# Row sums in the place of unread matmuls, and a second output piece that begins in another PSUM bank

## The chip, the cores and the metric

The kernel runs on one core of a Trainium2 chip. The core has four compute engines that this text names: TensorE (PE; its weight loads are PEld), VectorE (DVE), ScalarE (ACT) and GpSimd (POOL). SyncE (SP) issues most of the DMAs. The metric is the time of one execution in microseconds (us) on the device.

## The reference

Two computations follow one another. The first is a gated recurrence over 5056 tokens, for 4 sequences and 256 channels. The second is a soft mixture of experts on all 4 x 5056 = 20224 resulting tokens, with 8 experts of 4 slots, so 32 slots.

```
f = lower_bound + (1 - lower_bound) * sigmoid(f_logit)
h[t] = f[t] * h[t-1] + (1 - f[t]) * x[t]          # per sequence and channel
logits = h @ phi                                  # 20224 x 32
slot_input = softmax(logits over tokens).T @ h    # 32 x 256
slot_out[e] = relu(slot_input[e] @ w1[e]) @ w2[e] # 256 -> 1024 -> 256
out = softmax(logits over slots) @ slot_out       # 20224 x 256
```

The inputs x and f_logit have 20.7 MB each, the weights of the experts 16.8 MB in all, and the output has 20.7 MB. All of them are float32.

## The kernel before

The tokens of each sequence are cut into 10 groups (`n_grp`) of up to 512, so that 40 units (`n_unit`) of one group of one sequence arise. The order of all instructions is written out by hand (`tc.manual_schedule()`): each engine works through its own instructions in that order, and waits only for the data that it needs.

The loop over the units (from line 471) is a software pipeline. It loads six units ahead on SyncE's queue (L202 to L216). ScalarE takes the sigmoid (L226), GpSimd multiplies it with x (L237), TensorE transposes both to channels (L246 to L258), ScalarE makes the decay (L286, L293), and VectorE runs the recurrence as a scan (L304). TensorE transposes the result back to tokens (L317), VectorE or ScalarE copies it (L334), and TensorE forms the logits (L348). ScalarE takes their exponential into `etall` (L357), which stays in SBUF for the whole kernel, with a row for each sequence and slot and a column for each token. After a transpose of these weights (L369, copied in L372) TensorE sums the weighted tokens into `slot_ps` (L398). GpSimd's queue issues the 16 loads of the experts' weights along the way, at units that `W_AT` lists (L130, L140). These loads convert to bfloat16. The last two experts' `w2` go into a buffer of `f_t` (the tile `w_t`), and the very last comes in three parts: a half and two quarters.

In several places the loop calls `idle(k)` (L171): k matmuls of the 128 x 128 identity with 256 columns, which write into the second half of the bank of `slot_ps`. Nobody reads what they write. `spin(dst, k, w)` (L143) does the like with k matmuls of w columns of the first expert's weights. It is called after the loop, and writes into `tail[:, 1]`.

`tail` (L528) is a PSUM tile of 2 x 512 float32, so of two banks of 2 KB each. Its first bank holds `rs_ps`, the sums over the 32 slots for each token, and in the kernel before also `sin_ps`. Its second bank holds two transposes that are done by then, and the unread results of `spin`.

`row_sums(i)` (L377) is a matmul per 128 tokens, of the weights with four columns of ones (`ones`), and gives the denominators of the second softmax. The tokens of a sequence lie in blocks for it: two blocks of 2048 tokens (16 matmuls each) and one of 896 (7 matmuls), and 64 tokens are left over, for which L384 has a matmul of its own.

After the loop come the experts. `slot_sb` is a copy of `slot_ps` (L583). L587 brings it to channels in `sin_ps`. VectorE and ScalarE scale it into `sin` (L598, L599), TensorE multiplies with `w1` (L615), and ScalarE and VectorE apply the relu (L620, L622). TensorE transposes (L630); the first four experts go through `hid` (L651), the last four through `wide` (L664, a loop over j). Within this last loop the row sums are formed, and VectorE inverts them into `rrow` (L674, L680, L681). The scaled slots are `slot_out` (L683, L684) and `slot_bd` (L686).

The output stage multiplies `etall` with the slots. `pieces` (L714) treats the first 2048 tokens of sequence 0 in small pieces, so that the first store can start early: in each pair of pieces VectorE divides one (`by_vector`, L694) and ScalarE the other (`by_scalar`, L698), and each is then stored (L730). The sizes are (1, 2), (3), (2), counted in rows of 256 floats. For each entry of the list there is a new pair of PSUM tiles `op` of two banks each, and the pieces of one entry follow one another in the same tile, at the place `at`. `couple` (L744), `rest` (L770) and `whole` (L733) treat the remaining output in larger parts.

Of the kernel before, what the change touches and what calls it, by code (L numbers as in the profile page):

```python
# [18 lines left out]
def kernel(  # L19
# [11 lines left out]
    B, S, D = x.shape  # L31
    E = moe_w1.shape[0]
    F = moe_w1.shape[2]
    NS = moe_phi.shape[1]
    SPE = NS // E
    P = 128
    DC = D // P
    FC = F // P
    R = 4
    G = P * R  # L40
# [19 lines left out]
    wide_r = 4 * R  # L60
# [84 lines left out]
            nc.tensor.matmul(dst[:, ds(0, w)], w1_sb[0][:, 0, :P], w1_sb[0][:, 0, :w],  # L145
                             start=True, stop=True, skip_group_check=True)

    SPINS = 7
    W_AT = {9: 1, 17: 1, 25: 1, 31: 1, 32: 1, 33: 2, 34: 3, 36: 6}
    w_next = [0]  # L150
    ctx.enter_context(tc.manual_schedule())
# [4 lines left out]
    with tc.tile_pool(name="sp2", bufs=3) as sp2, \  # L156
# [217 lines left out]
            for i, k in enumerate(gs):  # L374
                ets[k] = et[:, i]

        def row_sums(i):  # L377
            t0, n_r = blocks[i]
            ew = etall[:, ds(t0, P * n_r)].rearrange("s (p r) -> s p r", r=n_r)
            for r in range(n_r):  # L380
                nc.tensor.matmul(rs_ps[:, t0 // P + r], ew[:, :, r], ones,
                                 start=True, stop=True, skip_group_check=True)
            if i == len(blocks) - 1:
                nc.tensor.matmul(rs_ps[:, n_grp * R - 1, ds(0, B // 2)],  # L384
                                 left.rearrange("s t u -> s (t u)"), pair_ones,
                                 start=True, stop=True, skip_group_check=True)
# [84 lines left out]
        for n in range(n_unit):  # L471
            if n < SINGLE - 2:
                if n:
                    unit(to_tokens, n - 1)
                    unit(u_to_channels, n + 1)
                s_to_channels(n + 2)
                if n + 3 < SINGLE:
                    gate(n + 3, 1)
                decay(n + 2, 1)
                if n + 3 == SINGLE:  # L480
                    gate(n + 3)
                if n % 2 == 0:
                    unit(load, n + AHEAD)
                unit(enter, n + 3)
                rep_constants(n)
            else:
                end = n >= n_unit - 6
                if n % 2 == 0:
                    unit(load, n + AHEAD)
                    if n == SINGLE - 2:  # L490
                        to_tokens(n - 1)
                        keep_tokens(n - 1)
                    if not end and n >= SETTLED:
                        unit(gate, n + 4)
                else:
                    unit(decay, n + 1)
                    if n < SETTLED:
                        gate(n + 3)
                    if n == n_unit - 5:
                        gate(n + 3)  # L500
                        exps(odd - 1)
                if not end and n != n_unit - 7:
                    group(exps, n - 2)

                unit(enter, n + 3)
                for _ in range(W_AT.get(n, 0)):
                    load_w(w_next[0])
                    w_next[0] += 1

                if n == n_unit - 2:  # L510
                    unit(u_to_channels, n + 1)
                if n != SINGLE - 2:
                    unit(to_tokens, n - 1)
                if n == n_unit - 2:
                    keep_tokens(n - 1)
                if n % 2 == 0:
                    unit(s_to_channels, n + 2)
                    unit(s_to_channels, n + 3)
                if n != n_unit - 2:
                    unit(u_to_channels, n + 1)  # L520
                if n in (n_unit - 5, n_unit - 4):
                    idle(8)
                elif n == SINGLE - 2:
                    idle(4, True)
                elif n < n_unit - 4 and n % (2 * B) in (1, 5, 6, 7):
                    idle({6: 8, 7: 9}.get(n, 5 if n % 2 else 4))
                if n == n_unit - 2:
                    tail = psp.tile([P, 2, G], F32, name="tail", tag="sp")  # L528
                    rs_ps = tail[:, 0, ds(0, n_grp * R * B)].rearrange(
                        "p (q b) -> p q b", b=B)  # L530
                    late_ps, odd_ps = (
                        tail[:, 1].bitcast(BF16)[:, ds(i * R * P, R * P)].rearrange(
                            "p (r s) -> p r s", r=R) for i in range(2))
                    logits(odd)
                    exps(odd)
                    slots(odd - 1)
                    spin(tail[:, 1], 1, G)
                    odd_weights()
                elif not end and long(n - 1):
                    if n % B == 0:  # L540
                        g = (n - 1) // (2 * B) * 2
                        for i in range(2):
                            logits(g + i, [2, 3] if n % (2 * B) == 0 else [0, 1])
                elif not end:
                    group(logits, n - 1)
            if n == n_unit - 1:
                logits(last, [0, 1, 2])
                late_exps([0, 1, 2])
                idle(4)
                late_weights([0, 1, 2], nc.scalar.copy)  # L550

            unit(scan, n)
            if n not in (SINGLE - 2, n_unit - 2):
                unit(keep_tokens, n - 1)
            if n == n_unit - 3:
                weights_to_tokens(odd - 1)
                slots(odd - 2)
            elif not n >= n_unit - 6:
                group(weights_to_tokens, n - 3)
                batch(slots, n - 4, 0)  # L560
                batch(slots, n - 4, 1)
                if n > 2 * B and n % (2 * B) == 3:
                    idle(6)
        hid, wide = (ld.tile([P, 2, R, D], F32, name=i, tag="x_t") for i in ("hid", "wide"))
        hid = hid.rearrange("p u r d -> p (u r d)").bitcast(BF16)[:, ds(0, FC * E // 2 * NS)]
        wide = wide.rearrange("p u r d -> p (u r d)").bitcast(BF16)[:, ds(0, FC * E // 2 * P)]
# [10 lines left out]
        slots(odd)  # L577
        late_slots([0, 1, 2])
        late_slots([3])
        spin(tail[:, 1], 21, P // 2)  # L580
        slot_sb = hpool.tile([P, G, DC], BF16, name="slot_sb", tag="h")
        slot_sb = slot_sb.rearrange("p t o -> p (t o)").bitcast(F32)[:, ds(0, D)]
        nc.vector.tensor_copy(slot_sb, slot_ps)  # L583
        sin_ps = tail[:, 0, ds(G // 2, DC * NS)].rearrange("p (o s) -> p o s", o=DC)
        slot_v = slot_sb.rearrange("p (c o) -> p o c", o=DC)
        for o in range(DC):
            nc.tensor.matmul(sin_ps[:, o], slot_v[:, o], rep[:, 0],  # L587
# [2 lines left out]
    with tc.tile_pool(name="ew", bufs=1) as ew, \  # L590
# [2 lines left out]

        rep2 = rep.rearrange("p b s -> p (b s)")

        spin(tail[:, 1], 21, P // 2)
        sin = ew.tile([P, DC, NS], BF16, name="sin")
        nc.vector.tensor_scalar_mul(sin[:, 0], sin_ps[:, 0], omlb[:, ds(0, 1)])  # L598
        nc.scalar.activation(sin[:, 1], sin_ps[:, 1], ACT.Copy, scale=omlb[:, ds(1, 1)])  # L599
# [61 lines left out]
        for j in range(Q):  # L661
            for fc in range(FC):
                for c in range(2):
                    nc.tensor.matmul(so_ps[c], wide[:, fc, j].rearrange("p b s -> p (b s)"),  # L664
                                     w2_sb[Q + j][:, fc, ds(c * C, C)],
                                     start=j == 0 and fc == 0,
                                     stop=j == Q - 1 and fc == FC - 1,
                                     skip_group_check=True)
            if j == 0:
                for c in range(2):  # L670
                    nc.tensor.matmul(so_ps[c], rep2, so4[:, ds(c * C, C)], start=False,
                                     stop=False, skip_group_check=True)
                row_sums(0)
                nc.vector.reciprocal(rrow[:, :wide_r], rs_ps[:, :wide_r])  # L674
            if j == 1:
                for i in range(1, len(blocks)):
                    row_sums(i)
                q = n_grp * R - 1
                spin(tail[:, 1], SPINS, D)
                nc.vector.reciprocal(rrow[:, wide_r:q], rs_ps[:, wide_r:q])  # L680
                nc.vector.reciprocal(rrow[:, q, ds(0, B // 2)], rs_ps[:, q, ds(0, B // 2)])  # L681
        spin(tail[:, 1], 4, D)
        nc.vector.tensor_scalar_mul(slot_out[:, ds(0, C)], so_ps[0], rcs)  # L683
        nc.scalar.activation(slot_out[:, ds(C, C)], so_ps[1], ACT.Copy, scale=rcs)  # L684
        for u in range(2):
# [4 lines left out]
    with tc.tile_pool(name="pout", bufs=4, space=PSUM) as pout, \  # L690
# [23 lines left out]
        def pieces(i, b, sizes):  # L714
            dst = rows_of(i, b)
            obs = [osb.tile([P, blocks[i][1], D], F32, name="ob", tag="ob") for _ in range(2)]
            r = 0
            for pair in sizes:
                ops = [pout.tile([P, R, D], F32, name="op", tag="op") for _ in range(2)]
                at = [0, 0]  # L720
                for k in pair:
                    todo = []
                    for j in range(2):
                        share(ops[j][:, ds(at[j], k)], i, b, r, k)
                        todo.append((r, at[j]))
                        r, at[j] = r + k, at[j] + k
                    for j, by in enumerate((by_vector, by_scalar)):
                        q, o = todo[j]
                        by(obs[j][:, ds(q, k)], ops[j][:, ds(o, k)], scale_of(i, b, q, k))
                        (nc.scalar if q == 1 else nc.sync).dma_start(  # L730
                            out=dst[:, ds(q, k)], in_=obs[j][:, ds(q, k)])
# [95 lines left out]
```

## Time and profile before

| | |
|---|---|
| runs | 200.14, 200.83 and 200.80 us; median 200.8 us |
| span of the profiled execution, first to last instruction | 198.1 us |
| its whole time | not given by the page; the runs lie 2.0 to 2.7 us above the span |
| busy: PE, DVE, ACT, POOL | 77%, 72%, 70%, 52% of the span |
| mean granted TensorE clock | 0.850 |
| DMA | 70.77 MB, mean 357 GB/s |
| chain that ended last, by engine | PE 32%, DMA 30%, DVE 18%, POOL 6% |
| `idle`, the 122 of 256 columns | 17.7 us of PE time (L174) |

The page divides the span into 40 slices, and gives the busy share of each engine and of the DMA engines in tenths, and the clock that TensorE was granted. The chain is followed back from the last instruction, at each step to what released it. A line of the timeline has the start, the length, the engine, the line of the kernel, the operation, the tiles, the number of instructions, and in brackets how long the engine had been idle and what ended that. In a line of waits stand the waiting engine and line, the one waited for, and then the total, the count and the longest in us.

### The profile page before, as it was taken

The numbers are of one execution on the slowest core, as the hardware profiler recorded it, in microseconds if no ns is written. First come the engines' busy times: TensorE is split into PE (matmuls) and PEld (weight loads), VectorE is DVE, ScalarE is ACT, GpSimd is POOL, SyncE is SP. The second block draws the span as 40 slices with busy tenths as digits, with TensorE's granted clock in tenths as the row PEclk, the third lists the DMA queues.
The fourth block names the chain that finished last, engine by engine and source line by source line (L and its number), as shares of the span: only waits on it lengthen the run. The fifth ranks groups of instructions, "written<-read, shape, count | busy, mean of one in ns | idle before, by whom it ended". The sixth has DMA issues, their size and how long they took to land.

```text
span 198.1 us, 3497 instructions
## 1 busy us (share of the span) xinstructions
PE 153.3 (77%) x1330; PEld 110.4 (56%) x1330; DVE 143.3 (72%) x164; ACT 138.7 (70%) x195; POOL 103.0 (52%) x78
## 2 busy tenths in 40 slices
PE   0587599987999989898997978999989999950000
PEld 0366478776776768676695856568953543310000
DVE  1669869999699999999989999523268878840000
ACT  2688677899889999999897595622069889980000
POOL 2489578774998688884969969290030000000000
PEclk9999759997999999999999999999995555555555
DMA  5999999999999999999999999999639999999995
GB/s 177 418 420 419 427 429 429 427 427 357 378 424 424 408 337 420 432 411 307 407 420 392 241 215 214 213 212 211 110 110 419 430 421 427 450 443 424 424 424 218
DMA packets 14448, 70.77 MB, mean 357 GB/s; under 512 B 1744, under 2 KB 3024, under 8 KB 10464
## 3 DMA queue, kind: packets, MB, share of 16 engines
q1 hardware_dynamic: 11520, 62.00, 75.5%
q0 software_dynamic: 2624, 8.42, 21.3%
q8 instruction: 10, 0.16, 0.3%
q10 hardware_dynamic: 288, 0.13, 0.2%
q14 instruction: 6, 0.05, 0.1%
HBM read 58.23 MB, written 20.71 MB: 399 GB/s over the span
## 4 chain that ended last, share of the span: by engine, by line
PE 32%; DMA 30%; DVE 18%; POOL 6%; issue 3%; ACT 1%; ACTq 0%; SPq 0%; POOLq 0%
DMA x_t<-in_x_dram 15%; DVE h L304 13%; PE op L754 12%; DMA w_t<-in_moe_w_dram 8%; DMA w_sb<-in_moe_w_dram 7%; POOL u_t L237 5%; PE hp L317 4%; PE up L258 4%; PE sp L252 3%; DVE ht L334 3%; PE op L704 2%; PE slot_ps L174 2%; PE lg L348 1%; PE slot_ps L398 1%; DVE ob L694 1%
## 5 line engine op out<-in xcount | busy, mean ns | idle before, releaser
L237 POOL TENSOR_TENSOR u_t<-s_t,x_t 128x1024 bf16<-128x1024 bf16 (+1 forms) x39 | 82.5, 2128 | 23.3 <-ACT s_t L226 13.9
L304 DVE TENSOR_TENSOR_SCAN h<-a,h,up 128x512 bf16<-128x512 f32 (+1 forms) x72 | 86.9, 1252 | 4.7 <-PE up L258 2.5
L226 ACT ACTIVATE s_t<-f_t 128x2048 bf16<-128x2048 f32 (+2 forms) x23 | 38.3, 1668 | 5.8 <-DMA f_t<-in_f_logit_dram 4.5
L317 PE MATMUL hp<-ident_f,h 128*128 128x128 f32 (+1 forms) x160 | 29.5, 309 | 7.3 <-DVE ht L334 6.0
L317 PEld LDWEIGHTS hp<-ident_f,h 128*128 128x128 f32 (+1 forms) x160 | 23.1, 208 | 15.3 <-DVE ht L334 9.6
L252 PE MATMUL sp<-ident_f,s_t 128*128 128x128 f32 x144 | 22.6, 303 | 10.1 <-ACT s_t L226 7.8
L286 ACT ACTIVATE a<-sp,nomlb 128x1024 f32<-128x1024 bf16 x24 | 25.4, 1114 | 0.8 <-PE sp L252 0.6
L252 PEld LDWEIGHTS sp<-ident_f,s_t 128*128 128x128 f32 x144 | 18.6, 158 | 11.8 <-issue 6.0
L754 PE MATMUL op<-slot_bd,etall 64*128 64x512 bf16 x62 | 24.4, 600 | 0.1
L765 ACT ACTIVATE oc<-op,rrow 128x256 f32<-128x256 f32 x60 | 22.8, 490 | 1.4 <-PE op L754 0.9
L759 DVE TENSOR_TENSOR oc<-op,rrow 128x1024 f32<-128x1024 f32 x16 | 19.3, 1223 | 4.6 <-PE op L754 4.5
L293 ACT ACTIVATE a<-sp,nomlb 128x512 f32<-128x512 bf16 (+2 forms) x22 | 17.9, 859 | 4.8 <-PE sp L252 4.4
L258 PE MATMUL up<-ident_f,u_t 64*128 64x64 f32 x192 | 17.6, 229 | 2.0 <-POOL u_t L237 1.9
L174 PE MATMUL slot_ps<-rep,ident 128*128 128x256 bf16 x122 | 17.7, 281 | 0.0
L258 PEld LDWEIGHTS up<-ident_f,u_t 64*128 64x128 f32 x192 | 13.9, 138 | 5.9 <-POOL u_t L237 2.4
L754 PEld LDWEIGHTS <-etall 64*128 64x128 bf16 x62 | 9.0, 153 | 14.2 <-issue 11.6
L334 ACT COPY ht<-hp 128x512 f32<-128x512 f32 (+1 forms) x18 | 10.4, 580 | 8.0 <-PE hp L317 7.9
L334 DVE COPY ht<-hp 128x512 f32<-128x512 f32 (+1 forms) x22 | 14.7, 668 | 0.8 <-PE hp L317 0.8
L174 PEld LDWEIGHTS <-ident 128*128 128x128 bf16 x126 | 11.4, 102 | 3.4 <-issue 1.3
L304 DVE TENSOR_TENSOR_SCAN h<-a,up 128x512 bf16<-128x512 f32 x8 | 9.3, 1209 | 2.5 <-ACT a L293 1.8
L252 PE MATMUL up<-ident_f,u_t 128*128 128x128 f32 x48 | 9.8, 337 | 0.6 <-POOL u_t L237 0.6
L348 PE MATMUL lg<-h,phi 128*32 128x512 bf16 (+1 forms) x80 | 10.0, 411 | 0.0
(105 smaller groups left out, 147.8 us busy)
## 6 DMA issues: line engine op xcount, KB each, us to landing
f_t<-in_f_logit_dram SPq DMA_DIRECT2D x12, 1024.0 KB, 12.3
x_t<-in_x_dram SPq DMA_DIRECT2D x12, 1024.0 KB, 11.4
out_dram<-oc SPq DMA_DIRECT2D x6, 2048.0 KB, 13.1
w_sb<-in_moe_w_dram POOLq DMA_DIRECT2D x14, 512.0 KB, 10.3
f_t<-in_f_logit_dram SPq DMA_DIRECT2D x12, 512.0 KB, 8.6
x_t<-in_x_dram SPq DMA_DIRECT2D x12, 512.0 KB, 9.4
out_dram<-oc SPq DMA_DIRECT2D x4, 896.0 KB, 6.1
out_dram<-ob SPq DMA_DIRECT2D x1, 2048.0 KB, 8.9
```

Of the source, the lines that this page charges most:

```text
L174: nc.tensor.matmul(slot_bank[:, 1, ds(0, rhs.shape[1])], ident, rhs, start=first and i < 2, stop=False, skip_group_check=True)
L226: nc.scalar.activation(s_t, f_t, ACT.Sigmoid, scale=-1.0)
L237: nc.gpsimd.tensor_tensor(uts[n][:, :r], s_t[:, :r], x_t[:, :r], ALU.mult)
L252: nc.tensor.transpose(ps[:, :, r], t[:, r], ident_f)
L258: nc.tensor.transpose(v[:, :, r], t(r)[k].bitcast(F32), ident_f[k, k])
L286: nc.scalar.activation(a, sp[:, :, :, :, o], ACT.Identity, scale=nomlb[:, ds(o, 1)], bias=1.0)
L304: nc.vector.tensor_tensor_scan(h[:, :T, o], decays[n // 2, o][:, n % 2, :T], up[:, :T, o], hs[number(g - 1, b)][:, ds(used(g - 1) - 1, 1), ...
L317: nc.tensor.transpose(hp[:n_p, r], hw[:, :n_p, r], ident_f)
L334: copy(hts[g][:n_p, b].rearrange("p r d -> p (r d)").bitcast(F32), hps.pop(n)[:n_p].rearrange("p r c -> p (r c)"))
L754: nc.tensor.matmul(op[:, i_r].rearrange("p u d -> p (u d)"), ew[:, :, r + i_r], slot_bd[ds(j * 2 * NS, 2 * NS)].rearrange("s u d -> s (u d)"),
L759: nc.vector.tensor_tensor(ob[:, :, ds(r, k)].rearrange("p u r d -> p r u d"), op[:, ds(0, k)], scale[:, ds(r, k)].unsqueeze(3).broadcast_t ...
L765: nc.scalar.activation(ob[:, u, r + i_r], op[:, i_r, u], ACT.Copy, scale=scale[:, r + i_r, ds(u, 1)])
```

## The change

Fewer matmuls with unread results: `idle` loses 25 in the loop, the two calls of `spin` with 21 matmuls each go, `SPINS` goes from 7 to 4 and the last `spin` from 4 to 2, where each matmul now has 512 (`G`) instead of 256 (`D`) columns. That makes 25 + 42 + 3 + 2 = 72.

`row_sums` takes a range. The sixteen of block 0 (2048 tokens) move into the places of the two calls of `spin`, eight into each; those of block 1 (2048 tokens) go where block 0's were; after them remains block 2 with the left-over. `sin_ps` moves from `tail[:, 0]` to `tail[:, 1]`.

In `pieces` a piece with an odd number of rows now takes one row more of its tile, so that the next one begins at an even row: the pieces of (1, 2) begin at 0 and 2 instead of 0 and 1, and each row of 256 floats is half a bank.

```diff
-    SPINS = 7
+    SPINS = 4
...
-        def row_sums(i):
+        def row_sums(i, rs=None):
...
-            for r in range(n_r):
+            for r in rs or range(n_r):
...
                 if n in (n_unit - 5, n_unit - 4):
-                    idle(8)
+                    idle(6)
...
-                    idle({6: 8, 7: 9}.get(n, 5 if n % 2 else 4))
+                    idle({6: 8, 7: 8}.get(n, 4 if n % 2 else 3))
...
                 if n > 2 * B and n % (2 * B) == 3:
-                    idle(6)
+                    idle(4)
...
-        spin(tail[:, 1], 21, P // 2)
+        row_sums(0, range(0, wide_r // 2))
...
-        sin_ps = tail[:, 0, ds(G // 2, DC * NS)].rearrange("p (o s) -> p o s", o=DC)
+        sin_ps = tail[:, 1, ds(0, DC * NS)].rearrange("p (o s) -> p o s", o=DC)
...
-        spin(tail[:, 1], 21, P // 2)
+        row_sums(0, range(wide_r // 2, wide_r))
...
-                row_sums(0)
+                row_sums(1)
                 nc.vector.reciprocal(rrow[:, :wide_r], rs_ps[:, :wide_r])
             if j == 1:
-                for i in range(1, len(blocks)):
+                for i in range(2, len(blocks)):
                     row_sums(i)
                 q = n_grp * R - 1
-                spin(tail[:, 1], SPINS, D)
+                spin(tail[:, 1], SPINS, G)
...
-        spin(tail[:, 1], 4, D)
+        spin(tail[:, 1], 2, G)
...
-                        r, at[j] = r + k, at[j] + k
+                        r, at[j] = r + k, at[j] + k + k % 2
```

## The prediction

> **What bounds the kernel now.** I read the page first (DMA line, clock line, chain), then the chain piece by piece after 100 us, then the timeline and the waits from 128 to 150 us, then stretches that follow the clock.
>
> From the page, the span in 40 slices of 4.95 us:
>
> ```profile
> PEclk9999759997999999999999999999995555555555
> DMA  5999999999999999999999999999639999999995
> ```
>
> The DMA engines are full from the second slice on, but for two slices, the 29th and 30th (digits 6 and 3, 139 to 149 us). So the time is: loads until the last weights land, a hole, stores until the end. Only the hole and its edges can move the end. The chain shows the left edge:
>
> ```profile
> 113.81 14.12 DMA w_sb<-in_moe_w_dram
> ...
> 128.21 15.66 DMA w_t<-in_moe_w_dram
> 143.88 0.04 issue
> 143.92 0.38 PE so_ps L664 x4
> 144.30 0.45 PE tail L145 x4
> ```
>
> The last quarter of the last expert's weights lands at 143.88, by a queue that was full for 15 us before. The timeline around it (start, length, line, what ended the wait):
>
> ```profile
> 139.87 1.48 PE L381 MATMUL tail<-ones,etall 128*128 128x4 bf16 x23
> ...
> 141.23 0.92 PE L145 MATMUL tail<-w_sb 128*128 128x256 bf16 x7
> 141.99 1.73 PE L664 MATMUL so_ps<-w_t,wide 128*128 128x128 bf16 x28
> 143.92 0.38 PE L664 MATMUL so_ps<-w_t,wide 128*128 128x128 bf16 x4 [0.20 <-DMA w_t<-in_moe_w_dram]
> ...
> 145.73 1.90 PE L704 MATMUL op<-slot_out,etall 32*128 32x256 bf16 x14 [0.50 <-DVE ob L694]
> ```
>
> TensorE arrives only 0.2 us early. Its 28 matmuls step by 0.056 us (1.73 less 0.2 of latency, over 27), so they need 1.57 us and could start at 143.92 - 1.57 = 142.35 instead of 141.99: the compute path has **0.36 us of slack**.
>
> **The change, part by part.** All is measured against the profiled span, 198.1 us; the median of the runs is 2.7 us above it, the lowest run 2.0, and I carry differences over to the median.
>
> 1. *25 `idle` matmuls fewer in the loop* (11 places from 5 to 4, three from 4 to 3, one from 9 to 8, three from 6 to 4, two from 8 to 6). Eight take 1.04 us at 113.46, a step of 0.107 us, so 2.7 us of TensorE work goes, 0.1 to 0.2 us at a place. VectorE is busy in nearly all of 56 to 125 us and the DMA engines in all of it, so they hide this: 0. Nobody reads the result. If the cover were gone the gain would be 0.1 to 0.2 us at a place that is on the chain.
>
> 2. *The two fillers of 21 become two times 8 row sums.* 21 fillers took 0.79 us; of row sums, 16 took 1.09 and 23 took 1.48, so one step is 0.056 us and eight take 0.64. The first filler hides behind the copy to slot_sb (ends 130.30, next matmul 130.36): 0. Behind the second waits VectorE's sin: -0.14 us on the compute path. The moved sums read weights written long before and issue no DMA; they pass no queue but TensorE's own.
>
> 3. *Row sums after the matmuls:* block 1's sixteen replace block 0's (0); then 7 and the left-over instead of 23 and it, 16 x 0.058 (L381 from 139.87 to L384 at 141.20) = -0.92 us.
>
> 4. *Filler of 7 x 256 becomes 4 x 512.* By the 256-column step, 7 x 0.107 = 0.75 against 8 x 0.107 = 0.85: +0.09. The last, 4 x 256 to 2 x 512, has the same columns: 0. It ends at 144.75 beside slot_out (ACT 144.34 + 0.37 = 144.71).
>
> Parts 2 to 4: -0.14 - 0.92 + 0.09 = **-0.97 us** for TensorE. What is late next is the weights, at 141.63, 142.62, 143.24 and 143.88 by the trace's landings, and these don't move. So the 0.97 goes into slack: 0.36 + 0.97 = 1.33 us. To the end: 0.
>
> 5. *The second piece on a bank of its own.* The 0.50 us wait before L704 above is TensorE, with 13 more matmuls and the first L754 behind it, waiting until VectorE has read piece one. If the wait goes, piece two starts at about 145.29, and with it VectorE's next copy, the stores and the end: at most -0.44. But does it go? The two pieces don't overlap now either, so what makes it wait is how finely the program tracks a PSUM tile. The waits of VectorE from 128 to 150 us:
>
> ```profile
> DVE rrow L680 <- PE tail L145: 2.5, 1, 2.5
> ...
> DVE sin L598 <- PE tail L145: 1.4, 1, 1.4
> ```
>
> rrow L680 reads row sums in `tail[:, 0]`, the fillers write `tail[:, 1]`, another 2 KB bank; yet it started at 142.19, just after the fillers' end at 142.15, not after the row sums' at 141.36. sin did the same (fillers end 131.63, sin starts 131.74). The whole tile is waited for, whichever bank. `op` is also one tile of two banks. Bounds: -0.44 (banks are told apart) to 0 (tile); I take 0, the nearer row. The new slot has no cost: the same copies of the same sizes.
>
> 6. *The clock.* The fillers did something after all. The trace's clock changes at 22.76, 29.59, 46.66, 50.07 and 149.06 us, all whole multiples of 3.413 us apart. A stretch of 3.413 us at full clock can send 8192 columns (0.107 us for 256). I summed each stretch's matmuls: columns, times the part of the 128*128 array in use, fp32 transposes twice (they step 0.112 us for 128 columns). Three full-clock stretches end in a drop, at shares of 0.25, 0.39 and 0.28; the lowest that keep the clock are 0.42 and 0.44. So below about 0.40 the next stretch has half the clock. The stretches themselves:
>
> ```profile
> 43.24:46.65 3.41, 2.21 (x32) 1.88 (x36) 2.94 (x4) 3.39 (x5) 2.67 (x2) 1.00 1.01 423
> 125.16:128.57 3.41, 2.96 (x24) 1.40 (x24) 1.34 (x2) 2.35 (x7) 0.89 (x2) 1.00 1.08 216
> 128.57:131.98 3.41, 3.06 (x82) 2.68 (x82) 0.89 (x4) 0.49 (x1) 3.41 (x3) 1.00 1.06 213
> ...
> 145.64:149.05 3.41, 3.19 (x20) 2.25 (x20) 2.81 (x5) 2.84 (x9) 1.07 (x2) 1.00 0.60 215
> ```
>
> (The columns are TensorE busy, its weight loads, VectorE, ScalarE, GpSimd, clock, DMA share, GB/s.) The first and last lost the clock after them, though TensorE was 65% and 94% busy. In the third stand 32 slot matmuls of 256 columns on a quarter of the array (2048), 42 fillers of 64 (2688) and small ones: 0.60. Without the fillers it is 0.27, and 16 row sums of 4 columns add 0.01. So I expect **half the clock for the stretch after it**, in the expert matmuls. Sliding the stretches' start over 3.4 us, since nothing ties it to the kernel, 31 of 35 positions give such a drop near 130 us. Costs: one stretch at half speed loses at most 1.71 us of TensorE time, against 1.33 of slack: 0 to +0.38. I take 0, since L615 to L664 also wait for VectorE and ScalarE in it, which don't slow.
>
> The Trainium skill, "TensorE: Matmul & The Clock Gate", says under "Why this matters for your kernels" that the clock falls after idle gaps of more than about 3 us. By it there is no drop here, since row sums fill the places, and part 6 would be 0. The rows above, with no such gap, speak for occupied columns instead.
>
> Sum: 0 on the loads' end, 0 to +0.38 by the clock, -0.44 to 0 by the piece: 0 near enough, 198.1 of span, and a median at the middle of what is known, **200.7 us**.
>
> **Rivals.**
> - *The piece is released.* Against it the two VectorE waits; for it that the wait in the trace is for a read in the bank shared now. -0.44: 200.3.
> - *Compute is what is late in a typical run.* The median is 0.66 over the lowest run, and 0.36 us of slack is little. Then up to 0.97 comes off: 199.8. Against it, TensorE waited for the weights in this trace, and a lowest run at 200.14 leaves little below.
> - *Slower: half the clock for two stretches.* Place: L615 to L664, 130 to 141 us. To come back, a stretch must hold 0.40 while it can send only half as much; of the two that ran at half speed early on, that with 0.36 stayed and those with 0.45 and 0.48 came back. The 32 matmuls of L615 are 32 x 512 / 4 = 4096 columns, 0.50 if all fall in one stretch, less if they are cut. On paper about a third of the positions stay down. Two stretches lose up to 3.41 us, less 1.33 of slack: +2.1, 202.8. It decides from where the lag passes 1.33 us.
> - *More drops in the loop* from part 1: stretches at 0.48 to 0.50 (70.6, 91.0, 118.3 us) lose 0.03 to 0.06 each and stay over 0.40 in most positions. A drop at 46.66 cost VectorE about 1.7 us (3.32 of 5 us busy from 50 to 55), so one more is +0.4 past the slack. I put it with the slower rival.
>
> **How the numbers follow.** No change 0.52; piece released 0.14; compute late 0.08; clock stays down or falls more often 0.26. About 0.5% (1.0 us) is what a measurement can tell from no change. Of the released cases 0.05 pass it (with a lucky clock), of the compute-late ones 0.04: faster 0.09. Of the slow rival 0.24 pass it. Same: 0.67. Low end 200.14 - 0.44 = 199.7, which takes in the rivals below; high end 200.8 + 2.1 = 202.9, which leaves out three stretches.
>
> **What would show it.** The last weights at about 143.9 and TensorE waiting in front of them for longer, in several places from 141 on; L664's last four at 143.9. The 0.5 us wait before L704 still there (right) or gone (released). A clock of 0.5 somewhere in 130 to 136: if it is 1.00 throughout, part 6 is wrong; if it lasts past one stretch and L664's last four start after 144.3, the slow rival is right. I am wrong altogether if the weights land elsewhere, since I took the loads' end as fixed.

## The result, and the profile after

The kernel after takes 201.64 us (median; 201.10 to 203.02), beside 200.73 us (200.01 to 201.17) for the kernel before on the same chip. The ratio is 1.0058, with a 95% interval of 1.0041 to 1.0074. So the change costs some 0.9 us. The forecast was no change at 200.7 us; the time lies within the range, on the side that had 0.24.

The profiled execution of the kernel after took 201.1 us, with a span of 199.3, so 1.8 us lie around the span. The span before was 198.1: 1.2 us less.

From the page of the kernel after, the clock, the DMA share in slices of 4.98 us, and the queue that reads instructions (packets, MB, share):

```profile
PEclk9999759996999999999999999979995555555555
DMA  5999999999999999999999999999449999999992
...
q8 instruction: 10, 0.16, 0.3%
```

A digit of 7 stands in the 27th slice of the clock (129.6 to 134.6 us) where a 9 stood: the half clock that the prediction expected. The DMA line still has its full stretches, its hole (4 and 4) and its full stretch behind. But its last digit has gone from 5 to 2 in a span that is 1.2 us longer: the end has a thin tail. The third line is read further below.

*The left edge.* The chain of the kernel after, then its timeline at the same place:

```profile
125.88 18.04 DMA w_t<-in_moe_w_dram
143.91 0.04 issue
143.95 0.61 PE so_ps L664 x8
144.56 0.45 PE tail L145 x2
```

```profile
131.44 3.43 PE L615 MATMUL hi_ps<-w_sb,sin 128*32 128x512 bf16 x32 [0.42 <-DVE sin L598]
...
141.84 1.50 PE L664 MATMUL so_ps<-w_t,wide 128*128 128x128 bf16 x24
143.95 0.61 PE L664 MATMUL so_ps<-w_t,wide 128*128 128x128 bf16 x8 [0.61 <-DMA w_t<-in_moe_w_dram]
...
145.99 1.25 PE L704 MATMUL op<-slot_out,etall 32*128 32x256 bf16 x10 [0.50 <-DVE ob L694]
```

TensorE is early, as forecast: it waits 0.61 us for the weights instead of 0.20. L615 took 3.43 us under the half clock (2.08 before), which the earlier start of 0.60 us and the sixteen row sums fewer after the experts' matmuls have paid for: its first matmul on `w_t` starts at 141.84 instead of 141.99. The 0.50 us in front of L704 are still there. What differs is the weights: by the trace's landings the four transfers into `w_t` came at 140.30, 141.61, 143.91 and 144.07 us (before: 141.63, 142.62, 143.24, 143.88). With the third part late, eight matmuls are left to do where there were four, and the first store is issued at 146.00 instead of 145.75. That is 0.25 us of the 1.2.

*The stores.* The rest, 1.0 us, is lost behind the hole, where no edit of the change stands but the place of one piece. From the first store's issue to the last landing it takes 51.05 us before and 52.06 after. The DMA answers from 148 to 198 us, first before, then after (queue: packets, MB, share; then the stores: count, KB each, median us from issue to landing):

```profile
q1 hardware_dynamic: 2693, 20.35, 96.5%
q10 hardware_dynamic: 6, 0.01, 0.0%
...
out_dram<-oc SPq DMA_DIRECT2D x6, 2048.0 KB, 13.1
out_dram<-oc SPq DMA_DIRECT2D x4, 896.0 KB, 6.1
out_dram<-ob SPq DMA_DIRECT2D x1, 2048.0 KB, 8.9
```

```profile
q1 hardware_dynamic: 2730, 20.44, 97.0%
q8 instruction: 1, 0.02, 0.1%
...
out_dram<-oc SPq DMA_DIRECT2D x6, 2048.0 KB, 14.2
out_dram<-oc SPq DMA_DIRECT2D x4, 896.0 KB, 5.6
out_dram<-ob SPq DMA_DIRECT2D x1, 2048.0 KB, 10.5
```

Both kernels store the same, and the engines are as full. But after, one packet stands among the stores that is no data: q8, "instruction". By the trace's packets it is a read of 16384 B at 167.2 us, which occupies one DMA engine for 0.96 us; a store's packet of the same size takes 0.61. The seven stores of 2048 KB, all of which land after that read, take 1.0 to 1.5 us longer from issue to landing than before. The four of 896 KB, which have landed by 161.9 us, do not. How the stores end is seen in the DMA share from 195 to 199 us in steps of 0.1 us, before and after (a lone 3 is the packet of one engine of sixteen, written where it starts, and it lasts six steps):

```profile
DMA  3990003400000000000000000000000000000000
```

```profile
DMA  0099330070000030000030000000000000000000
```

Before, the last two packets start at 195.6 and 195.7. After, fifteen engines are about as early, and one goes on alone with a packet at 196.4 and another at 197.0. The last store lands just behind that lone engine: its last packet ends at 197.7 us and the store has landed at 198.06 (before: 196.3 and 196.80).

So the theory that the runs are to test (**F, fetches**): TensorE's instructions are read from memory in blocks, on the DMA engines that also carry the data. The trace has ten such reads in both kernels. The last two begin at 139.6 and 146.4 us before, and at 141.9 and 167.2 after. That 146.4 lies in the hole is seen in the DMA share before, from 145 to 149 us in steps of 0.1 us:

```profile
DMA  0000000300000050699999961008999995248999
```

The lone 5 is the read at 146.4 (the 3 ahead of it is a smaller read of the page's other instruction queue, q14); the first packet of a store stands behind it, at 146.6, though that store was issued at 145.75. From the first read to the tenth TensorE has executed 1155 matmul records before and 1148 after, about 128 for each read. (q14 reads at nearly the same places in both.) Take 72 matmuls away, and the same block is due later: the tenth read slid out of the hole, where it cost nothing, into the stores, where every engine is needed. The Trainium skill, "Runtime: NRT & Kernel Launch", under "Instruction fetch mechanics", states that the sequencer fills its memory in blocks of 16 KiB, 256 instructions, by a DMA queue of its own. The trace agrees: 128 matmuls with a weight load each are 256 instructions. The page adds that the cost is "mostly hidden". For TensorE it is: none of its waits in the answers above names it. For the engine that carries the read it is not.

The rivals: **C**, the half clock from 132.0 to 135.4 us, that the missing fillers let in; **B**, the new place of the second piece; **P**, the smaller number of fillers in any other way.

### The profile page after: what moved, and what is told of

The parts are those of the page before. It is cut to its first block, busy times and chain, and to the rows that moved or that the text cites. A ratio compares the mean times of both kernels' runs of the same rounds, so it can differ in the third digit from the quotient of the medians.

```text
span 199.3 us, 3353 instructions
## 1 busy us (share of the span) xinstructions
PE 151.1 (76%) x1258; PEld 106.9 (54%) x1258; DVE 143.3 (72%) x164; ACT 138.2 (69%) x195; POOL 103.2 (52%) x78
## 4 chain that ended last, share of the span: by engine, by line
PE 30%; DMA 26%; DVE 21%; POOL 6%; issue 3%; ACT 2%; SPq 1%; ACTq 0%; POOLq 0%; DVEq 0%
DVE h L304 17%; PE op L754 12%; DMA w_t<-in_moe_w_dram 9%; DMA x_t<-in_x_dram 7%; DMA w_sb<-in_moe_w_dram 6%; POOL u_t L237 5%; PE hp L317 4%; DMA f_t<-in_f_logit_dram 4%; PE sp L252 3%; DVE ht L334 3%; PE up L258 3%; PE op L704 2%; PE lg L348 1%; PE slot_ps L398 1%; DVE ob L694 1%
## 5 line engine op out<-in xcount | busy, mean ns | idle before, releaser
L174 PE MATMUL slot_ps<-rep,ident 128*128 128x256 bf16 x97 | 14.8, 280 | 0.0
L174 PEld LDWEIGHTS <-ident 128*128 128x128 bf16 x101 | 8.9, 101 | 3.0 <-issue 1.3
```

Source lines behind the costliest of these rows:

```text
L174: nc.tensor.matmul(slot_bank[:, 1, ds(0, rhs.shape[1])], ident, rhs, start=first and i < 2, stop=False, skip_group_check=True)
```

## The experiments

All ratios are to the kernel before, run on the same chip beside the kernel. First store, last landing and fetches are from the trace of one profiled execution, in us; "fetches" are the last two reads of the instruction queue, and a number in bold lies among the packets of the stores. In every other kernel the last read starts ahead of the first store's first packet. Only one execution of each kernel was profiled, so where the reads of its other runs fell is not known.

| kernel | matmul records | fetches | first store | last landing | between | ratio, 95% interval |
|---|---|---|---|---|---|---|
| before | 1330 | 139.6, 146.4 | 145.75 | 196.80 | 51.05 | 1 |
| after | 1258 | 141.9, **167.2** | 146.00 | 198.06 | 52.06 | 1.0058, 1.0041 to 1.0074 |
| bank_only | 1330 | 139.2, 145.6 | 145.65 | 196.76 | 51.11 | 1.0016, 0.9993 to 1.0040 |
| after_pad72 | 1330 | 141.1, 147.3 | 147.16 | 198.12 | 50.96 | 1.0004, 0.9980 to 1.0029 |
| before_fewer36 | 1294 | 140.6, **153.2** | 145.71 | 198.24 | 52.53 | 1.0094, 1.0061 to 1.0128 |
| after_wide | 1264 | 140.6, **164.8** | 145.51 | 197.44 | 51.93 | 1.0059, 1.0035 to 1.0082 |
| after_f32idle | 1213 | 139.2, 142.7 | 145.04 | 196.23 | 51.19 | 0.9975, 0.9949 to 1.0000 |
| after_f32idle_wide | 1219 | 137.7, 142.3 | 144.65 | 195.52 | 50.87 | 0.9983, 0.9960 to 1.0006 |
| own_tiles | 1330 | 138.9, 145.5 | 145.36 | 196.39 | 51.03 | 0.9995, 0.9975 to 1.0016 |
| all_three | 1219 | 137.8, 142.4 | 144.68 | 195.20 | 50.52 | 0.9936, 0.9917 to 0.9955 |
| before_100_behind | 1430 | 145.3, **181.7** | 145.41 | 197.99 | 52.58 | 1.0080, 1.0050 to 1.0110 |

### bank_only

The kernel before, with one line changed:

```diff
-                        r, at[j] = r + k, at[j] + k
+                        r, at[j] = r + k, at[j] + k + k % 2
```

> The kernel before with only the last edit: a piece with an odd number of rows takes one row more of its tile. Theory F (fetches): in the trace of the kernel after, the queue called q8 instruction reads 16384 B packets of about 0.96 us, one DMA engine each; the last of ten falls at 146.4 us in the kernel before (in the hole between the last weights and the first stores) and at 167.2 us in the kernel after (in the middle of the stores), because 72 fewer matmuls mean that TensorE reaches the same block of its instructions later. This kernel keeps the number of matmuls, so F expects the last fetch at 146.4 us and no change against the kernel before (ratio 0.998 to 1.002). Theory B (bank): the place of the second piece costs the microsecond: ratio 1.004 to 1.007. Both expect the wait for VectorE's division at L704 to stay at about 0.50 us, as in the kernel after, since the step that the prediction took says that the whole tile is waited for; if it goes, the ratio would be about 0.998.

No loss that can be measured, and B's 1.004 is the very end of the interval. The tenth fetch stays at 145.6. In the timeline of this kernel the wait is what it was:

```profile
145.64 1.53 PE L704 MATMUL op<-slot_out,etall 32*128 32x256 bf16 x12 [0.50 <-DVE ob L694]
```

### after_pad72

The kernel after, with this in idle:

```diff
+        extra = [72]
+
         def idle(k, first=False):
...
+            for _ in range(0 if first else min(4, extra[0])):
+                extra[0] -= 1
+                nc.tensor.matmul(slot_bank[:, 1, ds(0, 2)], ident, rep_bf[:, ds(0, 2)],
+                                 start=False, stop=False, skip_group_check=True)
```

> The kernel after with 72 more matmuls of 2 columns, four behind each call of idle but the first until the 72 are used up, so that as many TensorE instructions as in the kernel before stand ahead of the experts. Theory F (fetches) expects the last fetch back in the hole, at 145 to 147 us, no fetch in the stores, and a time like that of the kernel before: ratio to it 0.996 to 1.002, so about 1 us less than the kernel after. Theory C (clock): the half clock of 132 to 135.4 us, which the fewer filler columns let in, costs the microsecond. The 72 matmuls bring 144 columns in all, so the half clock should stay and with it the loss: ratio 1.004 to 1.007. Theory B (bank) expects the same 1.004 to 1.007, since that edit is kept.

72 matmuls that do nothing take the loss away: 1.0004. The clock was not what they mended. From the stretches of this kernel (us, TensorE busy, weight loads, VectorE, ScalarE, GpSimd, clock, DMA share, GB/s):

```profile
134.20:137.61 3.41, 3.41 (x34) 1.78 (x27) 1.39 (x2) 1.19 (x2) 0.15 (x1) 0.50 1.07 215
```

The half clock in the experts is there still. The first store is 1.4 us later than in the kernel before, since TensorE left the loop over the units 1.5 us later in this profile (its next matmuls start at 131.25 us, before at 129.74); what held it up there is not settled. This profiled execution is also the longest of its kernel (201.17 us where the median is 200.0), so its start of the stores is not the usual one. The stores themselves took 50.96 us, with the fetch at 147.3, just ahead of their first packet and 0.3 us later than F allowed. F holds; C and B fall.

### before_fewer36

The kernel before, in both places:

```diff
-        spin(tail[:, 1], 21, P // 2)
+        spin(tail[:, 1], 3, 7 * P // 2)
```

> The kernel before with each of its two calls of spin that have 21 matmuls of 64 columns made into 3 of 448 columns: as many columns, but 36 matmuls fewer; nothing else is changed. Theory F (fetches) expects the last fetch to leave the hole at 146.4 us and to fall into the stores, somewhere between 150 and 165 us, and a loss of 0.4 to 1.2 us: ratio 1.002 to 1.006. Theory C (clock) and theory B (bank) expect no loss: 0.998 to 1.001, since the array keeps its columns and the pieces their places.

As many filler columns, in 6 matmuls instead of 42, and nothing else: 1.0094. The fetch has left the hole. From the DMA answer from 148 to 198 us, and the end of the stores from 195 to 199 in steps of 0.1 us:

```profile
q1 hardware_dynamic: 2676, 20.33, 96.4%
q8 instruction: 1, 0.02, 0.1%
...
out_dram<-oc SPq DMA_DIRECT2D x4, 896.0 KB, 7.8
```

```profile
DMA  9300340000300000300000300000000000000000
```

Again one engine goes on alone, with packets at 196.0, 196.6 and 197.2. The clock was full from 49.8 to 148.8 us, so no half clock in the experts takes part in this loss. And the delay begins where the read falls: the four stores of 896 KB, issued from 151.1 to 154.2 us around the read at 153.2, take 7.8 us in the median instead of the 6.1 before, where in the kernel after, with its read at 167.2, they took 5.6. The direction is F's; the size is not. F expected 1.002 to 1.006, and the stores lasted 1.5 us longer, not the 0.99 that the read took.

### after_wide

The kernel after; the same stands behind the second eight row sums:

```diff
         row_sums(0, range(0, wide_r // 2))
+        spin(tail[:, 1, ds(P // 2, 7 * P // 2)], 3, 7 * P // 2)
```

> The kernel after with 3 matmuls of 448 unread columns behind the eight row sums at each of their two new places: 6 matmuls more, and the filler columns that the two calls of spin had in the kernel before. Theory C (clock) expects the stretch from 132.0 us to keep the full clock and the time to come back to that of the kernel before: ratio 0.998 to 1.001. Theory F (fetches) expects the full clock too, but the last fetch still in the stores (163 to 167 us) and the loss still there: ratio 1.003 to 1.007.

```profile
131.79:135.20 3.41, 3.25 (x47) 1.91 (x48) 1.68 (x5) 1.75 (x4) 2.06 (x5) 1.00 1.06 213
```

The clock is full (1.00) in the stretch that had half of it, and TensorE reaches its first matmul on `w_t` at 140.95 instead of 141.84. The first store goes out at 145.51, before that of the kernel after (146.00); by the trace that is because the last weights landed at 143.63 instead of 144.07, and TensorE waited for them in both. The time does not come back: 1.0059, the same as after. This is the run that separates C from F, since it mends the one and leaves the other: the fetch is at 164.8, in the stores.

### after_f32idle and after_f32idle_wide

The other way out of the stores: not more matmuls but fewer still, so that the tenth block is never due. The kernel after with this in idle; after_f32idle_wide has the two spins of after_wide too:

```diff
         def idle(k, first=False):
             rhs = ident if first else rep_bf
+            if not first:
+                while k > 1:
+                    w = min(k, 4) * (D // 8)
+                    nc.tensor.matmul(
+                        slot_bank[:, 1, ds(0, 2 * w)].rearrange("p (u d) -> p u d", u=2), ident_f,
+                        ident_f[:, ds(0, w)].unsqueeze(1).broadcast_to([P, 2, w]),
+                        start=False, stop=False, skip_group_check=True)
+                    k -= min(k, 4)
```

> The kernel after, with the 97 matmuls of idle that follow the first call made into 26 float32 matmuls of up to 256 columns of the identity (two passes of TensorE each): as many array cycles or so, but about 45 matmul records fewer than the kernel after. Theory F (fetches): the ninth fetch, at 141.9 us in the kernel after with some 1130 matmuls done, moves 45 matmuls on, to 144.5 to 146.5 us, past the last weights; the tenth would lie behind the last matmul and goes. So no fetch in the stores, one fewer among the last weights, and the loss of the kernel after gone: first store to last landing 51.0 us again, as in the three traces without a fetch in the stores (51.0 to 51.1), against 51.9 to 52.5 in the three with one. Ratio to the kernel before 0.996 to 1.002. Theory P (number of fillers): it was the missing matmuls themselves, by clock or by order, that cost the microsecond; then a kernel with fewer still stays slow: 1.004 to 1.010.

> As after_f32idle, and 3 matmuls of 448 unread columns behind the row sums at each of their two new places, which kept the full clock at 132 us in after_wide. Theory F (fetches): the ninth fetch at 144 to 146.5 us, no tenth; the experts' matmuls are done some 0.9 us earlier than in the kernel after, and if the ninth fetch was what the last weights waited for, these land up to 0.9 us earlier. Ratio to the kernel before 0.992 to 1.000. If the last weights land at 143.6 to 144.1 us all the same, their end does not hang on that fetch, and the ratio is 0.997 to 1.001. Theory P (number of fillers): 1.003 to 1.008.

Nine fetches in both, none in the stores, and the loss is gone: 0.9975 and 0.9983. P falls. C falls once more: after_f32idle has the half clock among the experts too, from 131.40 to 134.81 us, and after_f32idle_wide has not, and their ratios are alike. From the page of after_f32idle, then the queues of its DMA answer from 148 to 198 us, where q1 stands alone:

```profile
q8 instruction: 9, 0.15, 0.3%
```

```profile
q1 hardware_dynamic: 2596, 20.19, 95.6%
```

Two expectations missed their place. The ninth fetch was to come at 144.5 to 146.5 us and came at 142.7 and 142.3, since a fetch does not stand exactly at its multiple of 128: in the kernel before, the matmuls executed at the later nine reads are 3 to 53 more than the rule gives from the first. And the last weights landed at 142.49 and 142.77 us instead of 143.88, so by more than the 0.9 us allowed. Why they are early is seen in what the DMA engines moved from 140 to 146 us, in steps of 0.15 us, before and in after_f32idle:

```profile
GB/s 191 178 150 137 157 102 123 102 96 102 96 82 34 14 14 14 14 7 14 14 14 14 14 7 0 0 0 0 0 0 0 0 0 0 0 0 0 0 55 0
```

```profile
GB/s 198 198 171 164 137 103 116 123 103 96 68 61 55 21 7 0 0 109 0 0 0 0 0 0 0 0 0 0 0 0 0 0 0 55 0 0 0 0 0 212
```

Before, from 142 us on, 14 GB/s trickle for 1.6 us: by the packets, which follow one another every 0.08 us, that is what one engine moves, while the others have nothing to do. In after_f32idle the trickle is missing; the lone 109 is the ninth fetch itself, behind the weights. Before, two fetches (132.4 and 139.6) began between 128 and 142 us; in after_f32idle one (139.2), in after_f32idle_wide and all_three too (137.7, 137.8). In the eight traces with two, the last weights land at 143.5 to 144.1 us, in the three with one at 142.5 to 142.8. That agrees with a fetch each on the same DMA engine. In the kernel after, the ninth read lasts from 141.91 to 142.88, and no packet of the weights starts between 142.11 and 142.87; then the trickle goes on. But the packets do not name their engine, so this is argued and not shown.

The end gained little of that, since TensorE was what was late then: in after_f32idle its 32 matmuls on `w_t` run in one piece from 141.65, without a wait for the weights.

### own_tiles and all_three

The kernel before, with one line changed; all_three is after_f32idle_wide with the same line:

```diff
-        pieces(0, 0, [(1, 2), (3,), (2,)])
+        pieces(0, 0, [(1,), (2,), (3,), (2,)])
```

> The kernel before with the list of pieces (1,), (2,), (3,), (2,) in place of (1, 2), (3,), (2,): the piece of two rows has a pair of PSUM tiles of its own. It tests the step of the prediction that the second piece waits because the whole tile is waited for, and not for its bank. If that is so, the wait of 0.50 us for VectorE's division at L704 goes, and the second pair of stores is issued up to 0.44 us earlier (before: 1.0 us behind the first). What that is worth: 0 if the transfers are bound by what comes later, at most 0.44 us; ratio 0.997 to 1.001. If the wait stays, something else than the tile holds the piece.

> after_f32idle_wide with the list of pieces of own_tiles. If the gains are of different kinds they add up: the time is below that of after_f32idle_wide by what own_tiles gains, 0 to 0.44 us; ratio to the kernel before 0.990 to 1.000. If the second pieces only come earlier onto busy DMA engines, it equals after_f32idle_wide within 0.002.

With tiles of its own the second piece does not wait. The timeline of own_tiles:

```profile
144.41 1.97 PE L704 MATMUL op<-slot_out,etall 32*128 32x256 bf16 x14
...
146.72 0.37 PE L704 MATMUL op<-slot_out,etall 32*128 32x256 bf16 x2 [0.35 <-ACT ob L698]
```

Fourteen matmuls run in one piece where two and twelve stood with 0.50 us between them. The first store of the second pair, of 256 KB, follows the first store by 0.55 us instead of 1.11. In the kernel before no gain from that can be measured (0.9995, 0.9975 to 1.0016), and from the first store to the last landing it takes 51.03 us as against 51.05. all_three, at 0.9936, is the only version here whose interval lies wholly below the kernel before, by 1.3 us in the middle. Its ratio is 0.0047 lower than that of after_f32idle_wide (0.9983), some 0.9 us: more than the 0.44 us of the one expectation and more than the 0.002 of the other, so neither holds. Their intervals nearly touch, and whether the pieces gain more where the weights end early stays open.

### before_100_behind

The kernel before, with this at its end:

```diff
                     couple(i, j)
+        op = pout.tile([P, R, D], F32, name="op", tag="op")
+        for _ in range(100):
+            nc.tensor.matmul(op[:, 0, ds(0, 2)], etall[:, ds(0, P)], ones[:, ds(0, 2)],
+                             start=True, stop=True, skip_group_check=True)
```

> The kernel before with 100 matmuls of 2 unread columns behind the last matmul of the output stage; nothing waits for them, and everything ahead of them is as before. Theory F (fetches): the tenth fetch stays at 146.4 us, and an eleventh falls at about 177 us, where the last real matmuls end while the stores go on for 19 us; the stores last 0.9 to 1.4 us longer (51.0 to 51.1 us from the first store to the last landing without a fetch among them, 51.9 to 52.5 with one): ratio 1.004 to 1.008. If a fetch in the stores is harmless by itself and the loss of the kernel after came from fewer fillers ahead of them, the ratio is 0.998 to 1.002.

Everything ahead of the 100 matmuls is the kernel before, they take 2.83 us from 176.45 on, nothing waits for them, and the stores still have some 20 us to go. The ratio is 1.0080. Its page, and its end from 195 to 199 us:

```profile
q8 instruction: 11, 0.18, 0.3%
```

```profile
DMA  0990300400300300000300000000000000000000
```

An eleventh fetch, at 181.7 instead of the expected 177, and the stragglers of the kernels with a fetch in their stores. The last stores had all been issued by 178.2 us. The stores that land by 177.3 us are no slower than in the kernel before; the four that land later take 0.8 to 1.1 us longer from issue to landing. So it is the fetch that costs, not what stands ahead of the stores; it is shown with more matmuls as with fewer.

All eleven traces together: seven without a fetch in the stores need 50.5 to 51.2 us for them, four with one need 51.9 to 52.6. The fetch costs 0.9 to 1.5 us, where it occupies its engine for 0.95 to 0.99 (0.88 in before_100_behind). Why the price can be above that time is not settled.

## Why the prediction was wrong, point by point

- **What bounds the kernel.** "Only the hole and its edges can move the end": this is the step that failed. It takes the stores' length for fixed because their bytes are. They were 1.0 us longer, by a read of TensorE's instructions that had moved from 146.4 us in the hole to 167.2 us among the stores. Part 2's "they pass no queue but TensorE's own" is the same oversight: matmuls take up a DMA queue as well, that of their instructions. The queue stood on the page, as 0.3% of the engines' time. As a share it is nothing; but each of its 10 packets holds up one engine of sixteen for 0.88 to 0.98 us, and one of them among full engines cost 0.9 to 1.5 us here.
- **Part 1, idle.** 0, hidden by VectorE and the DMA engines. As TensorE time this was right to within 0.4 us: the work behind the loop began 0.44 us earlier in the kernel after (below), which may come from these matmuls or from the spread between executions, and it went into slack. But the text asked only what a matmul takes and who reads it. That it is also an instruction that must be fetched was missed, there and in parts 2 to 4, whose 47 fewer count alike.
- **Parts 2 to 4.** L615 started 0.60 us earlier, more than the 0.14 by which the filler shrank, since the first eight row sums already began 0.44 us before the filler that they replace (129.30 and 129.74); the row sums after the experts' matmuls were shorter by about the expected amount (7 at 140.61 in 0.49 us). So the gain was nearer 1.5 us than 0.97, and the 1.35 us that L615 lost to the half clock took most of it: the first matmul on `w_t` starts 0.15 us earlier. The wait for the weights grew by 0.41, which is due to their later landing as well.
- **The weights' landings.** "These don't move" was not quite right: in the profiled execution the third came 0.67 us later, and the first store 0.25. The ninth fetch lasted from 141.91 to 142.88, ahead of that landing, with no packet of the weights starting from 142.11 to 142.87. That fits F, but no run isolates it.
- **Part 5, the bank.** Right: 0.50 us before and after, since the tile is what is waited for; own_tiles shows it by the tile. With the wait gone the ratio is 0.9995, 0.9975 to 1.0016: no gain is shown, though the interval does not exclude the 0.44 us of the lower bound.
- **Part 6, the clock.** Right in place, length and price: full again after one stretch, from 132.00 to 135.41, 1.35 us lost in L615 where at most 1.71 was allowed, and nothing at the end (after_wide, 1.0059 with the full clock). The stretch of the kernel after ahead of the drop, in the columns used above:

```profile
128.59:132.00 3.41, 2.99 (x57) 2.31 (x52) 0.85 (x4) 0.32 (x2) 3.41 (x3) 1.00 1.05 211
132.00:135.41 3.41, 3.41 (x34) 1.43 (x27) 1.18 (x2) 1.19 (x2) 2.17 (x5) 0.50 1.06 214
```

  TensorE was busy for 2.99 of 3.41 us, and the clock fell. The rule of "TensorE: Matmul & The Clock Gate" in the Trainium skill, that it falls after idle gaps of over 3 us, would have kept it; the measurement decides for occupied columns. The bound of 0.40 is known only to some hundredths: in the kernel after, a stretch from 91.04 with a share of 0.38 to 0.41 kept the clock, and one from 43.26 with 0.35 to 0.38 lost it, depending on how a matmul across the border of a stretch is counted.
- **The rivals.** None of them is what happened. The piece was not released, compute was early, and the clock was low for one stretch more and no longer. The chance of 0.24 for slower was given to a mechanism that did not occur, so that the time lies within the range is luck.

## What to carry to other kernels

An instruction has a price apart from its duration: when blocks of instructions are read by the engines that move the data, the number of instructions decides where those reads fall. Before removing or adding some dozens of them, count them against the reads in the trace (here about one for each 128 matmuls with their weight loads), and see whether a read slides into a stretch where all DMA engines are full; a hole in the transfers is the place for it. And a stage whose bytes are fixed is not a stage whose length is fixed: look at whether its end is one engine that goes on alone.

## What the hardware showed that was not expected

- A read of 16384 B of instructions took 0.88 to 1.31 us, where a store's packet of the same size took 0.61, and one read among the stores made a stage of 51 us longer by 0.9 to 1.5 us, from the place where it fell onward.
- A fetch does not come the moment its count is reached: in before_100_behind the 100 matmuls had ended at 179.3 us, and the eleventh read began at 181.7, amid full queues. So its place can be told from the count only to some microseconds.
- At the end of the loads the last weights still came for 1.6 us at 14 GB/s, what one engine moves in packets of 1024 B one after another. With one fetch fewer between 128 and 142 us, the weights landed 1.1 to 1.4 us sooner than in the kernel before.
